# A scan kernel with an ELU layer behind it: B and C turned on VectorE instead of TensorE, one load for exp(cum), and other PSUM banks for the quarters of a product

## The chip, the cores and the metric

The kernel runs on one core of a Trainium2 chip. The core has five engines, each with a queue of its own that it works off in order: TensorE (PE in the profile; PEld is its weight load), VectorE (DVE), ScalarE (ACT), GpSimd (POOL) and SyncE (SP), which here only issues transfers. Products are written to PSUM, eight banks of 512 float32 values for each of 128 partitions; everything else lies in SBUF. The metric is the time of one execution on the device in microseconds (us).

## The reference

The input is `x` (4 batches, 8 heads, 768 positions, 32 channels), a decay `a` for each position, and `B` and `C` (16 states for each position). A scan runs along the positions, by chunks; its output of 3072 rows and 256 columns goes through two matrix products with an ELU between them. The weights come as float64.

```python
cum = np.cumsum(la, axis=-1)
L = np.exp(cum[:, :, :, None] - cum[:, :, None, :]) * causal
CB = np.einsum('bhin,bhjn->bhij', Cc, Bc)
y_intra = np.einsum('bhij,bhjd->bhid', CB * L, xc)
y_inter = np.einsum('bhin,bhnd->bhid', Cc, state) * np.exp(cum)[:, :, :, None]
y[:, :, sl] = y_intra + y_inter
Bx = np.einsum('bhjn,bhjd->bhjnd', Bc, xc) * np.exp(cum[:, :, -1:] - cum)[..., None, None]
state = np.exp(np.sum(la, axis=-1))[:, :, None, None] * state + np.sum(Bx, axis=2)
# then, on y as 3072 x 256:
h = x @ w_in                                            # 256 -> 2048
g = np.where(h > 0.0, h, np.exp(np.minimum(h, 0.0)) - 1.0)
return g @ w_out                                        # 2048 -> 256
```

## The kernel before

**Groups.** The 3072 rows are worked in 12 groups n of 256 positions, all 8 heads at once; groups 2p and 2p+1 are the same stretch of two batches and make a pair. For each group SyncE loads B and C into one tile `bc` (`load_bc`, line 106: four loads, positions on the partitions, eight heads of 16 states along the row) and `x` (`load_x`). From a table in DRAM it spreads exp(cum) over the partitions (`spread_exp`, line 340, tile `ec`: eight loads, one a head) and cum itself (`spread_cum`, tile `L`).

**The scan of a group.** `scaled` (line 357) multiplies B by a decay for the state's update. `turn` (line 368) transposes B and C with four products against the identity on TensorE into two PSUM tiles (`ps_tb`, `ps_tc`); ScalarE copies B to `bt`, VectorE writes C masked by head to `ctm`; `turn_exp` (line 385) writes C times exp(cum) to `cts`. `scores` multiplies them, `weigh` applies L, `sums` and `states` carry the state on, `across` and `inside` make y, which ScalarE copies to `yT`.

**The two layers.** The first four groups use plain products (`l1`, line 583, and `l2`, line 707). From group 4 on the two groups of a pair are taken together, and seven products stand for eight, by sums and differences of quarters (Strassen's scheme in Winograd's form). For each pair n and each of eight column blocks i of the hidden layer, three functions (lines 659 to 691, products at line 655) do so:

- `front`: three products of 128 x 256; ScalarE copies the first one out of PSUM (`p_copy`, line 665). `front_sums`: two sums on VectorE (lines 673, 674).
- `mid`: two products, one sum on VectorE (line 682).
- `back`: two products, two sums (lines 689, 690).

The results fill two PSUM tiles c1 and c2, each of two halves of 256 columns and one bank in size. Every product takes two passes of TensorE, so that the profile counts two records a product. The queue `lag` holds finished tiles for the ELU: `begin_elu` is relu of the negated value on ScalarE (line 596), `elu` adds exp on ScalarE (line 603) and max(e - 1, h) on VectorE (line 605, tile `g`), after which the bank is free. `sum_t1` and `sum_t2` on GpSimd form the differences of the quarters of g that the second layer needs.

`second(n)` is the second layer of a pair as 56 steps of two products of 128 x 128 (line 759), with sums on VectorE and GpSimd at line 750. The loop over k (two for each i) sets the order by hand: while the first layer of pair n runs, `l2s(count)` takes that many steps of the second layer of pair n-2 and lays them between front, mid and back: four steps after front, two after mid, one after back. `scan_ahead(n, i)` puts in the scan of the pair to come.

**PSUM.** Seven banks are one ring (`ps_a`), from which scores, states, y, turns, c1, c2 and half of the second layer's tiles are taken in turn; the eighth holds the rest. A tool of the language adds the waits between engines, and for PSUM it adds them between any two accesses of different engines to one bank.

Of the kernel before, what the change touches and what calls it, by code (L numbers as in the profile page):

```python
# [16 lines left out]
P = 128  # L17
# [11 lines left out]
def kernel(  # L29
# [76 lines left out]
    def load_bc(n, c_queue=nc.sync):  # L106
        b, g = place(n)
        st.setdefault(n, {})["bc"] = raw.tile([P, 2, 2, NH, N], F32, tag="bc", name="bc", bufs=2)
        for u in range(2):
            sl = slice((2 * g + u) * P, (2 * g + u + 1) * P)  # L110
            for k, src in enumerate((B, C)):
                (nc.sync, c_queue)[k].dma_start(  # L112
                    out=st[n]["bc"][:, k, u], in_=src[b, :, sl, :].rearrange("h s n -> s h n"))
# [226 lines left out]
    def spread_exp(n):  # L340

        st.setdefault(n, {})["ec"] = ec = att.tile([P, 2, P], F32, tag="ec", name="ec", bufs=4)
        for h in range(NH):
            row = rows_of(n).start + NG * h
            nc.sync.dma_start(
                out=ec[N * h:N * (h + 1)].rearrange("n u i -> n (u i)"),
                in_=flat_exp[row:row + 1].to_broadcast([N, BLK]))
# [11 lines left out]
    def scaled(n, eng):  # L359
# [5 lines left out]
            out=sc, in0=s["bc"][:, 0],  # L365
            in1=factor.unsqueeze(3).to_broadcast([P, 2, NH, N]), op=ALU.mult)

    def turn(n):
# [8 lines left out]
        s["bt"] = att.tile([P, 2, P], F32, tag="bt", name="bt", bufs=3)  # L377
# [7 lines left out]
    def turn_exp(n):  # L385
# [3 lines left out]
        nc.vector.tensor_tensor(out=s["cts"], in0=s.pop("ct"), in1=s["ec"], op=ALU.mult)  # L389
# [270 lines left out]
    def front(n, i):  # L660
# [5 lines left out]
        part_product(c2[:, 1], s_in[0][:, i], t[:, 1], True)  # L666
        part_product(c2[:, 0], a21[:, i], t[:, 0])
        open_[n, i] = c1, c2, copy

    def front_sums(n, i):  # L670
        c1, c2, copy = open_[n, i]
        u = conv.tile([P, 2, BLK], F32, tag="mag", name="u_sum")
        nc.vector.tensor_tensor(out=u[:, 0], in0=c2[:, 1], in1=copy, op=ALU.add)
        nc.vector.tensor_tensor(out=u[:, 1], in0=c2[:, 0], in1=u[:, 0], op=ALU.add)
        open_[n, i] = c1, c2, u

    def mid(n, i):
# [3 lines left out]
        part_product(c1[:, 1], s_in[1][:, i], y_sums[n][:, 2])  # L681
        nc.vector.tensor_tensor(out=c2[:, 1], in0=c1[:, 1], in1=u[:, 1], op=ALU.add)  # L682

    def back(n, i):
        c1, c2, u = open_.pop((n, i))
        b22 = yT[n // 2][:, 1, 1].rearrange("p u i -> p (u i)")
        part_product(c1[:, 1], a22[:, i], y_sums[n][:, 3])
        part_product(c2[:, 0], s_in[2][:, i], b22)
        nc.vector.tensor_tensor(out=c1[:, 1], in0=c1[:, 1], in1=u[:, 0], op=ALU.add)  # L689
        nc.vector.tensor_tensor(out=c2[:, 0], in0=c2[:, 0], in1=u[:, 0], op=ALU.add)  # L690
        lag.append((n, i, c1))
# [8 lines left out]
    def l2(n, j, half=None):  # L700
# [10 lines left out]
        if j == MC // 2 - 1 and half != 0:  # L711
            ob = ffn.tile([P, 2, DM], F32, tag="ob", name="ob")
# [11 lines left out]

    def sum_t1(n, i, eng=nc.gpsimd):
        b12 = g_of[n + 1, i][:, 0]
        eng.tensor_tensor(out=b12, in0=b12, in1=g_of[n, i][:, 0], op=ALU.subtract)  # L727

    def sum_t2(n, half):
        for i in range(4 * half, 4 * half + 4):  # L730
            t2_of[n, i] = ffn.tile([P, BLK], F32, tag="t2", name="t2", bufs=4)
            sub(t2_of[n, i], g_of[n + 1, i][:, 1], g_of[n + 1, i][:, 0])
# [3 lines left out]
    def second(n):  # L736
# [6 lines left out]
        for half in range(2):  # L743
# [8 lines left out]
            for r, a in enumerate((a11, a12, s1, s2, s3, a22, s4)):  # L752
                pool, tag = (p_a, "a") if (7 * half + r) % 2 else (p_o, "o")
                ps = pool.tile([P, 2, P], F32, tag=tag, name="ps_o")
                for i in chunk:
                    A, B = g_of[n, i], g_of[n + 1, i]
                    b = (A[:, 0], A[:, 1], B[:, 0], t2_of[n, i], A[:, 0], A[:, 1], B[:, 1])[r]
# [7 lines left out]
                if r == 0:  # L765
                    nc.scalar.copy(out=p1, in_=ps)
                    for i in chunk:
                        sub(g_of[n, i][:, 0], t2_of[n, i], g_of[n, i][:, 0])
                    if half:
                        add(c11, c11, p1)  # L770
                elif r == 1:
                    add(c11, ps, c11 if half else p1)
                    for i in chunk:
                        sub(g_of[n, i][:, 1], g_of[n, i][:, 1], t2_of[n, i])
# [139 lines left out]
    for s, (n, i) in enumerate((  # L914
# [14 lines left out]
        if s == 4:  # L929
            scaled(2, nc.gpsimd)  # L930
        if s == 5:
            turn(2)
            first_exp(2)
            turn_exp(2)
# [32 lines left out]
    def scan_ahead(n, i):  # L967
# [6 lines left out]
        if 4 <= m < NP and n % 2 == 0:  # L974
# [11 lines left out]
            if i in (5, 7):  # L986
                turn(m + i // 7)
                turn_exp(m + i // 7)
        if 4 <= m < NP and n % 2 == 1:
            if i == 0:  # L990
                scaled(m, nc.gpsimd)
                scaled(m + 1, nc.gpsimd)
            for k in (i,) if m == 4 else (i, i + 1) if i % 2 == 0 else ():
# [17 lines left out]
    for n in (2, 3):  # L1011
        for i in range(8):
# [11 lines left out]
            if n == 2:  # L1024
# [3 lines left out]
                if i == 1:  # L1028
                    scaled(3, nc.gpsimd)
                    turn(3)  # L1030
# [20 lines left out]
    for n in range(4, NP, 2):  # L1051
# [14 lines left out]
        for k in range(16):  # L1066
# [18 lines left out]
            elif m and i == 5:  # L1085
                l2s(2)
                mid(n, i)
                states(m)
                l2s(2)
                back(n, i)  # L1090
                states(m + 1)
                next_elu()
                begin_elu()
            else:
                mid(n, i)
                if i == 0 and n > 4:
                    store(n - 4, 0)
                    store(n - 4, 1)
                l2s(2)
                back(n, i)  # L1100

# [7 lines left out]
                next_elu()  # L1109
# [54 lines left out]
```

## Time and profile before

| | us |
|---|---|
| median of three runs (lowest, highest) | 366.25 (365.03, 367.19) |
| span of the profiled execution, first to last instruction | 362.9 |
| runs' median less this span | 3.35 |
| busy in it: TensorE | 354.3 |
| VectorE | 242.2 |
| GpSimd | 227.1 |
| ScalarE | 200.7 |

The profile shows one execution. The runs are timed on the device from outside, so that a few microseconds lie around the span. Stages, by the span: start and first groups to about 27 us, groups with plain first layer to 53, plain second and first layer to 117, the four pairs (n = 4, 6, 8, 10) to 334, and the second layer of the last pair to the end. In a row of the profile, `out<-in` are tiles, then shapes as partitions x elements, the count, busy time, the mean of one in ns, and the idle time of the engine before them with what ended it. A line of the chain has its start, its length and what ran.

### The profile page before, as it was taken

How to read it: one execution, taken by the hardware profiler on the slowest of the kernel's cores; microseconds unless marked ns; L12 is line 12 of the kernel's file. 1: busy time of each engine (PE TensorE's matmuls, PEld its weight loads, DVE VectorE, ACT ScalarE, POOL GpSimd, SP SyncE). 2: the span in 40 equal slices, each digit the busy share in tenths (PEclk: the TensorE clock that was granted, in tenths of full speed). 3: DMA queues.
4: the chain of work that ended last, by engine and by line, in shares of the span. 5: the costliest groups of instructions: out<-in, count | busy, mean ns of one | idle time of the engine just before them, and what ended most of it. 6: DMA issues, size and time to landing. Idle time of an engine off the chain costs nothing.

```text
span 362.9 us, 10146 instructions
## 1 busy us (share of the span) xinstructions
PE 354.3 (98%) x3978; PEld 316.9 (87%) x3978; DVE 242.2 (67%) x547; ACT 200.7 (55%) x499; POOL 227.1 (63%) x366
## 2 busy tenths in 40 slices
PE   8899999999999999999999999999999999999996
PEld 5578778888888998898999998999989999999995
DVE  4989887972697668784567684666685666666212
ACT  4858969767435567635485735386735352534100
POOL 4454443663567896679457578567587555456893
PEclk9999999999999999999999999999999999999999
DMA  8877995563050560053530045540000100000001
GB/s 155 203 203 147 240 308 141 66 116 63 3 116 19 65 85 12 4 115 48 96 65 2 3 95 68 93 72 0 3 2 4 58 2 0 3 0 32 29 2 58
DMA packets 96239, 25.33 MB, mean 70 GB/s; under 512 B 77312, under 2 KB 92096, under 8 KB 96192
## 3 DMA queue, kind: packets, MB, share of 16 engines
q1 hardware_dynamic: 94016, 24.49, 33.0%
q8 instruction: 31, 0.51, 0.6%
q10 hardware_dynamic: 2176, 0.20, 0.4%
q14 instruction: 16, 0.13, 0.1%
HBM read 21.33 MB, written 3.34 MB: 68 GB/s over the span
## 4 chain that ended last, share of the span: by engine, by line
PE 81%; DVE 7%; ACT 3%; DMA 3%; SPq 2%; issue 2%; POOL 1%; ACTq 0%; DVEq 0%
PE ps_o L759 32%; PE ps_h L655 25%; PE ps_h L583 10%; PE ps_o L707 8%; SPq L112 2%; PE ps_g L459 1%; DMA w<-in_moe_w_in_dram 1%; DVE g L605 1%; PE ps_y L553 1%; ACT e L596 1%; PE ps_st L489 1%; ACT e L603 1%; DMA flat<-F 1%; DVE mag L183 1%; PE ps_y L534 1%
## 5 line engine op out<-in xcount | busy, mean ns | idle before, releaser
L596 ACT ACTIVATE e<-ps_h 128x512 f32<-128x512 f32 x96 | 56.5, 588 | 93.1 <-DVE ps_h L689 71.2
L605 DVE SCALAR_TENSOR_TENSOR g<-e,ps_h 128x512 f32<-128x512 f32 x96 | 65.3, 681 | 39.2 <-ACT e L603 35.8
L759 PEld LDWEIGHTS ps_o<-w_out,g 128*128 128x128 f32 x640 | 80.3, 192 | 3.3 <-issue 0.5
L759 PE MATMUL ps_o<-w_out,g 128*128 128x128 f32 x640 | 81.4, 275 | 0.0
L727 POOL TENSOR_TENSOR g<-g 128x256 f32<-128x256 f32 x34 | 24.8, 729 | 67.1 <-DVE g L605 67.1
L583 PE MATMUL ps_h<-yT,w_in 128*128 128x256 f32 x256 | 60.6, 383 | 2.5 <-POOL w_in L200 1.8
L603 ACT ACTIVATE e<-e 128x512 f32<-128x512 f32 x96 | 60.9, 634 | 2.2
L583 PEld LDWEIGHTS ps_h<-yT,w_in 128*128 128x128 f32 x256 | 47.8, 190 | 10.6 <-POOL w_in L200 2.8
L759 PE MATMUL ps_o<-w_sum,g 128*128 128x128 f32 x320 | 43.0, 275 | 0.0
L759 PEld LDWEIGHTS ps_o<-w_sum,g 128*128 128x128 f32 x320 | 41.1, 192 | 1.4
L439 ACT ACTIVATE L<-L,ncum 128x64 f32<-128x64 f32 x160 | 41.0, 338 | 0.0
L655 PE MATMUL ps_h<-y_sum,w_in 128*128 128x256 f32 x128 | 38.6, 383 | 0.7 <-DVE ps_h L682 0.7
L655 PE MATMUL ps_h<-y_sum,w_sum 128*128 128x256 f32 x128 | 38.5, 382 | 0.5 <-DVE g L605 0.5
L655 PE MATMUL ps_h<-yT,w_in 128*128 128x256 f32 x128 | 38.8, 385 | 0.0
L444 POOL TENSOR_SCALAR_AFFINE_SELECT L<-L 64x512 f32<-64x512 f32 x40 | 27.3, 682 | 13.1 <-ACT L L439 11.8
L707 PE MATMUL ps_o<-w_out,g 128*128 128x256 f32 x128 | 30.8, 383 | 0.0
L655 PEld LDWEIGHTS ps_h<-y_sum,w_sum 128*128 128x128 f32 x128 | 23.9, 190 | 5.3 <-DVE g L605 1.3
L723 POOL TENSOR_TENSOR g<-t,g 128x256 f32<-128x256 f32 x40 | 27.9, 729 | 0.8 <-PE ps_o L759 0.8
L723 POOL TENSOR_TENSOR t<-g 128x256 f32<-128x256 f32 x40 | 28.1, 736 | 0.2
L723 POOL TENSOR_TENSOR g<-g,t 128x256 f32<-128x256 f32 x40 | 27.9, 730 | 0.2
L707 PEld LDWEIGHTS ps_o<-w_out,g 128*128 128x128 f32 x128 | 23.7, 190 | 3.4 <-POOL L L444 0.2
L689 DVE TENSOR_TENSOR ps_h<-ps_h,u_sum 128x256 f32<-128x256 f32 x32 | 13.7, 429 | 18.3 <-PE ps_h L655 18.3
(109 smaller groups left out, 538.3 us busy)
## 6 DMA issues: line engine op xcount, KB each, us to landing
L<-flat SPq DMA_DIRECT2D x20, 256.0 KB, 5.3
w<-in_moe_w_in_dram SPq DMA_DIRECT2D x8, 512.0 KB, 5.2
w<-in_moe_w_out_dram SPq DMA_DIRECT2D x8, 512.0 KB, 6.1
xr<-in_x_dram SPq DMA_DIRECT2D x24, 128.0 KB, 3.4
out_dram<-c_sum SPq DMA_DIRECT2D x10, 256.0 KB, 2.1
bc<-in_B_dram SPq DMA_DIRECT2D x24, 64.0 KB, 4.4
bc<-in_C_dram SPq DMA_DIRECT2D x22, 64.0 KB, 3.4
ec<-flat_exp SPq DMA_DIRECT2D x72, 16.0 KB, 1.7
```

The lines of the kernel that those rows point to most:

```text
L439: nc.scalar.activation(L[:, h, u], L[:, h, u], ACT.Exp, bias=ncum[:, u, row:row + 1])
L444: nc.gpsimd.affine_select(out=part, in_=part, pattern=[[0, 4], [0, 2], [1, Q]], compare_op=ALU.is_ge, fill=0.0, base=0, channel_multiplier=-1)
L583: nc.tensor.matmul(out=ps[:, j], lhsT=w_in[:, k, m * P:(m + 1) * P], rhs=yT[n // 2][:, k, n % 2].rearrange("p u i -> p (u i)"), start=(k = ...
L596: nc.scalar.activation(begun[0], lag[0][2], ACT.Relu, scale=-1.0)
L603: nc.scalar.activation(e, e, ACT.Exp, scale=-1.0)
L605: nc.vector.scalar_tensor_tensor(out=g_of[n, i], in0=e, scalar=1.0, in1=ps, op0=ALU.subtract, op1=ALU.max)
L655: nc.tensor.matmul(out=out, lhsT=lhsT, rhs=rhs, start=first, stop=True, skip_group_check=True)
L689: nc.vector.tensor_tensor(out=c1[:, 1], in0=c1[:, 1], in1=u[:, 0], op=ALU.add)
L707: nc.tensor.matmul(out=o_of[n][:, ts], lhsT=g_of[n, j][:, m % 2, ts * P:(ts + 1) * P], rhs=w_out[:, m], start=(m == 0 and ts == 0), stop=( ...
L723: nc.gpsimd.tensor_tensor(out=out, in0=in0, in1=in1, op=ALU.subtract)
L727: eng.tensor_tensor(out=b12, in0=b12, in1=g_of[n, i][:, 0], op=ALU.subtract)
L759: nc.tensor.matmul(out=ps[:, ts], lhsT=b[:, ts * P:(ts + 1) * P], rhs=a[:, i], start=(i == chunk[0] and ts == 0), stop=(i == chunk[-1]), s ...
```

## The change

It has four parts.

1. **Turning.** For groups 2 to 11, B and C are loaded so that each run of 8 positions x 16 states of one head is a row of 512 bytes on one partition, and one VectorE operation (`turn_square`, a transpose within squares of 32 x 32) for each of B and C makes the turned tile `bct` out of it. B in the old layout is loaded as well, for `scaled`. `mask_heads` and `turn_exp` follow as VectorE steps of their own, read SBUF in place of PSUM, and are spread over the steps by `turn_part`. Groups 0 and 1 keep `turn`.
2. **exp(cum)** comes by one load a group in place of eight.
3. **Banks.** front's second product goes to the second half of c1 in place of c2; mid's second and back's first product go to c2, the sums write the other way, and back's two sums become one over the whole of c2. c1 is then whole after mid. `quarters` tells which half of g is which quarter.
4. **Order.** c1's ELU begins after mid and ends before back, c2's begins after back.

```diff
+        if n > 1:
+            st[n]["b"] = raw.tile([P, 2, NH, N], F32, tag="b", name="b_tok", bufs=2)
+            for u in range(2):
+                sl = slice((2 * g + u) * P, (2 * g + u + 1) * P)
+                nc.sync.dma_start(
+                    out=st[n]["b"][:, u], in_=B[b, :, sl, :].rearrange("h s n -> s h n"))
...
+            for k, src in enumerate((B, C)):
+                for m in range(2):
+                    nc.sync.dma_start(
+                        out=squares[:, k, m],
+                        in_=src[b, m:NH:2, g * BLK:(g + 1) * BLK, :].rearrange(
+                            "q (c t) n -> q c (t n)", t=8))
+            return
...
-        for h in range(NH):
-            row = rows_of(n).start + NG * h
-            nc.sync.dma_start(
-                out=ec[N * h:N * (h + 1)].rearrange("n u i -> n (u i)"),
-                in_=flat_exp[row:row + 1].to_broadcast([N, BLK]))
+        nc.sync.dma_start(
+            out=ec.rearrange("p u i -> p (u i)"),
+            in_=flat_exp[rows_of(n)].unsqueeze(1).to_broadcast([NH, N, BLK]))
...
+    def turn_square(n, k):
...
+        nc.vector.transpose(
+            out=s["squares"][:, k].rearrange("p u i -> p (u i)").rearrange("p (c t) -> p t c", t=8),
+            in_=s["bc"].rearrange("p k u h n -> p k (u h n)").rearrange(
+                "p k (m t n) -> p k t m n", m=2, n=N)[:, k])
...
+    def turn_part(n, part):
+        if part < 2:
+            turn_square(n, 1 - part)
+        elif part == 2:
+            mask_heads(n)
+        else:
+            turn_exp(n)
...
         copy = conv.tile([P, BLK], F32, tag="sgn", name="p_copy")
         nc.scalar.copy(out=copy, in_=c1[:, 0])
-        part_product(c2[:, 1], s_in[0][:, i], t[:, 1], True)
-        part_product(c2[:, 0], a21[:, i], t[:, 0])
+        part_product(c1[:, 1], s_in[0][:, i], t[:, 1])
+        part_product(c2[:, 1], a21[:, i], t[:, 0], True)
...
-        nc.vector.tensor_tensor(out=u[:, 0], in0=c2[:, 1], in1=copy, op=ALU.add)
-        nc.vector.tensor_tensor(out=u[:, 1], in0=c2[:, 0], in1=u[:, 0], op=ALU.add)
+        nc.vector.tensor_tensor(out=u[:, 0], in0=c1[:, 1], in1=copy, op=ALU.add)
+        nc.vector.tensor_tensor(out=u[:, 1], in0=c2[:, 1], in1=u[:, 0], op=ALU.add)
...
-        part_product(c1[:, 1], s_in[1][:, i], y_sums[n][:, 2])
-        nc.vector.tensor_tensor(out=c2[:, 1], in0=c1[:, 1], in1=u[:, 1], op=ALU.add)
+        part_product(c2[:, 0], s_in[1][:, i], y_sums[n][:, 2])
+        nc.vector.tensor_tensor(out=c1[:, 1], in0=c2[:, 0], in1=u[:, 1], op=ALU.add)
+        lag.append((n, i, c1))
...
-        part_product(c1[:, 1], a22[:, i], y_sums[n][:, 3])
-        part_product(c2[:, 0], s_in[2][:, i], b22)
-        nc.vector.tensor_tensor(out=c1[:, 1], in0=c1[:, 1], in1=u[:, 0], op=ALU.add)
-        nc.vector.tensor_tensor(out=c2[:, 0], in0=c2[:, 0], in1=u[:, 0], op=ALU.add)
-        lag.append((n, i, c1))
+        part_product(c2[:, 0], a22[:, i], y_sums[n][:, 3])
+        part_product(c2[:, 1], s_in[2][:, i], b22)
+        nc.vector.tensor_tensor(
+            out=c2, in0=c2, in1=u[:, 0].unsqueeze(1).to_broadcast([P, 2, BLK]), op=ALU.add)
         lag.append((n + 1, i, c2))
...
-            ob = ffn.tile([P, 2, DM], F32, tag="ob", name="ob")
+            ob = ffn.tile([P, 2, DM], F32, tag="ob", name="ob", bufs=1)
...
-            if i in (5, 7):
-                turn(m + i // 7)
-                turn_exp(m + i // 7)
+            if i > 2:
+                turn_part(m + i // 6, i % 3)
...
                 mid(n, i)
...
+                begin_elu()
                 l2s(2)
+                next_elu()
                 back(n, i)
-
+                begin_elu()
...
                 l2s(1)
-                next_elu()
-                begin_elu()
```

## The prediction

> **What bounds the kernel now.** I read the page first: engine shares, then the chain that ended last.
>
> ```profile
> PE 354.3 (98%) x3978; PEld 316.9 (87%) x3978; DVE 242.2 (67%) x547; ACT 200.7 (55%) x499; POOL 227.1 (63%) x366
> ...
> PE 81%; DVE 7%; ACT 3%; DMA 3%; SPq 2%; issue 2%; POOL 1%; ACTq 0%; DVEq 0%
> ```
>
> TensorE (PE) is busy almost throughout and carries 81% of the chain; the shares of VectorE, ScalarE and GpSimd are an average with slack. A busy PE is not yet a PE at its pace, so the chain in order of time comes next, for one turn of the loop over i in the stage of pairs (117 to 334 us, 32 turns).
>
> ```profile
> 180.41 1.30 PE ps_h L655 x6
> 181.71 1.78 PE ps_o L759 x16
> 183.50 0.87 PE ps_h L655 x4
> 184.36 0.89 PE ps_o L759 x8
> 185.25 0.87 PE ps_h L655 x4
> 186.56 1.30 PE ps_h L655 x6
> ```
>
> A turn is 6.15 us (186.56 - 180.41): front's three products 1.30 (0.43 each, two records a product), eight L759 products 1.78, mid's two 0.87, four L759 0.89, back's two 0.87, two L759 0.44. The parts add up to the turn, so PE has no gap in it. Anything put between two PE products here lengthens the kernel one for one. What stands around PE is in the timeline.
>
> ```profile
> 178.94 0.60 PE L655 MATMUL ps_h<-y_sum,w_in 128*128 128x256 f32 x2
> 179.38 0.59 PE L655 MATMUL ps_h<-yT,w_sum 128*128 128x256 f32 x2
> 179.58 0.43 DVE L689 TENSOR_TENSOR ps_h<-ps_h,u_sum 128x256 f32<-128x256 f32 x1 [0.89 <-PE ps_h L655]
> 180.04 0.60 ACT L596 ACTIVATE e<-ps_h 128x512 f32<-128x512 f32 x1 [2.23 <-DVE ps_h L689]
> 180.25 0.60 PE L655 MATMUL ps_h<-yT,w_in 128*128 128x256 f32 x2
> 180.67 0.63 ACT L603 ACTIVATE e<-e 128x512 f32<-128x512 f32 x1
> 180.69 0.59 PE L655 MATMUL ps_h<-y_sum,w_sum 128*128 128x256 f32 x2
> 181.21 0.58 ACT L596 ACTIVATE e<-ps_h 128x512 f32<-128x512 f32 x1
> 181.69 0.36 ACT L665 COPY p_copy<-ps_h 128x256 f32<-128x256 f32 x1
> ```
>
> The front starts at 180.25, its second product at 180.69. The copy of the first product (L665) stands on ScalarE behind relu, exp, relu and runs from 181.69 to 182.05: 1.36 us after the second product began. Today nobody on PE needs it before mid, 1.78 us of products later; that cover is what the change has to keep or lose. Three more views give prices: the timeline at a turn of B and C, the timeline at a wait, and two groups of the page or of the list by line.
>
> ```profile
> 135.85 0.38 PE L374 MATMUL ps_tb<-ident,bc 128*128 128x128 f32 x2
> 136.06 0.38 PE L374 MATMUL ps_tc<-ident,bc 128*128 128x128 f32 x2
> ...
> 142.20 0.70 PE L655 MATMUL ps_h<-y_sum,w_in 128*128 128x256 f32 x2 [0.67 <-DVE ps_h L682]
> ```
>
> ```profile
> L665 ACT COPY p_copy<-ps_h 128x256 f32<-128x256 f32 x32 | 11.8, 369 | 6.2 <-PE ps_h L655 6.1
> ...
> L750 DVE TENSOR_TENSOR c_sum<-ps_o,c_sum 128x256 f32<-128x256 f32 x20 | 8.4, 421 | 12.2 <-POOL c_sum L750 10.5 <-PE ps_o L759 1.7
> ```
>
> The copy takes 0.37 us in the mean; some of VectorE's L750 sums sat waiting for GpSimd, 10.5 us in all. The next PE work after the four transposes starts at 136.28, so a group's transposes take 0.43 us of PE. After a wait PE restarts 0.53 us before its next product (142.20, 142.73) where 0.43 is usual: 0.1 us of uncovered weight load per wait.
>
> **What the Trainium skill says.** "PSUM — Partial Sum Buffer", section "PSUM bank collisions raise a hardware error": two engines must not touch one bank in the same 32 partitions at once, whatever the addresses, so waits belong to the bank. The trace of before doesn't show such a wait apart (its c1[:, 0] products wait for the copy of the same half), but the changed program's waits follow it. "Perfetto Trace Analysis", section "Optimizing Tensor Performance", Matmuls: rotate independent groups through different banks so that evacuation overlaps the next matmuls; the trace agrees: copy in c1, second product in c2, no gap. "VectorE: DVE Perf Modes", section "The three transpose paths": VectorE turns 32x32 blocks only, 311 ns for 128x128 bf16. No square transpose is in the trace.
>
> **The change part by part.** Sums are made against the profiled execution: span 362.9 us. The runs' median is 366.25, 3.35 more, for what lies around the span; I add that at the end.
>
> 1. Banks in front. Before: c1[:, 0], ScalarE copies it, c2[:, 1], c2[:, 0]. After: c1[:, 0], copy, c1[:, 1], c2[:, 1]. The second product now writes the bank that ScalarE reads. In the changed program's queue this product waits for p_copy (L707 there), in all 32 fronts, and nothing stands on PE between first product and wait. Behind it on PE queue two front products and everything later.
> When does the copy end? ScalarE's order in after: relu(c1), exp(c1), relu(c2), copy. VectorE's: mid's sum, g(c1), back's sum. Count from the start of mid's second product: mid's sum starts at 0.63 (183.77 to 184.40 in the timeline), 0.43 long: 1.06. relu 0.03+0.60: 1.69. exp 0.03+0.63: 2.35. g(c1) starts 2.38; back's one sum of 128x512 stands behind it and starts 0.60 later (an independent VectorE operation overlaps by 0.08): 2.98. Its length isn't shown; L605 and L381 of that size take 0.68, two halves 0.86 at most: I take 0.68: 3.66. relu(c2) at 3.69, copy 0.48 after it (181.21 to 181.69): 4.17, ends 4.54, PE goes on at 4.59.
> PE reaches that product after 0.43+0.89+0.87+0.44+0.43 = 3.06. Stall 1.53 us. The 1.36 above, with the old order of the ELU, bears out its size.
> The 32 fronts (n = 4, 6, 8, 10, eight i each; all but n=10 have scan work for the next pair): i=1 to 4 always, 16; i=0 for n=6, 8, 10, since the ring runs on from the pair before; i=5 to 7 for n=10; i=7 for n=8, whose inside falls in an even step: 23 ordinary x 1.53 = 35.2. Three (i=6 with scan work) lack the two L759 products before the front: 1.97 x 3 = 5.9. Three (i=5) have 2 to 3 us of scores, sums and L759 ahead, only the turn-round is left: 0.2+0.37+0.05 = 0.62 x 3 = 1.9. Two (i=7, n=4 and 6) follow the yT copies on ScalarE, six of 0.32: 1.7 x 2 = 3.4. The first of all, behind one ELU: 1.3. Sum 47.7. The p5 copy falls between relu and exp about five times, 0.3 each: 1.5. Restart 0.1 x 32 = 3.2. Together 52.4. Mid's products gain waits too: c1[:, 0] for L715 and c2[:, 0] for L716, which read the same banks. VectorE ends L716 about 1.5 us after the second front product starts, PE comes there at 0.87+1.78 = 2.65: covered, with 1.1 us to spare, so nothing is taken; without that margin it would add one for one. What is late next is the whole of PE: the stall comes back each turn, and VectorE, ScalarE and GpSimd wait with it. The last L759 stage (334 us to the end) has no front and keeps its length.
>
> 2. PE transposes gone for groups 2 to 11: 10 x 0.43 = -4.3. The stalls of PE that came right after turns or late copies (0.83, 0.43, 0.36, 0.21, 0.15 by the starts of PE's records) disappear in the larger ones: -2.0. The bt copies (0.36, ScalarE, after exps) were hidden.
>
> 3. Squares: 20 more VectorE operations of 256 elements. The nearest row is 0.42 (L673); bounds 0.31 and 1.0. In odd steps they stand behind back's sum, inside the new stall. In even steps VectorE has front's sums to about 1.5, g to 2.1, up to two L750 sums to 3.0, and mid's sum is due at 3.72: 0.45 fits, 1.0 would cost some 0.3 us in the six even steps that hold one (two per scanned pair), +2. Before the pairs (40 to 80 us, VectorE 17 to 18.6 of 20) four squares, 1.7 us, less one cts moved to GpSimd: I take +0.5, bounds -0.4 and +1.7. A square that waited for a late load would hold VectorE; loads are issued at k=0 and 1, used from k=3, over 6 us later, and land in 3.7 us.
>
> 4. SyncE: per group 4 loads and 8 of ec become 6 and 1. Fewer issues by queue order, B loaded twice; they end earlier (L112 at 25 us held the queue 4.30 us, but PE was without gaps from 27.5 to 38.2). Nothing. ob single: its two uses lie 30 us apart.
>
> 5. back's two sums become one (0.86 to 0.68) and c1's ELU starts at mid: counted in 1.
>
> Sum: 362.9 + 52.4 - 4.3 - 2.0 + 0.5 = 409.5, and 3.35 outside the span: 413.
>
> **Rivals.** A, ordinary but short stall: ScalarE reaches the copy at once, as in the i=5 fronts; 32 x (0.62+0.1) = 23, so 362.9+23-5.8+3.35 = 383. For it: ScalarE is only 55% busy. Against: relu(c2) stands ahead of the copy and depends on back's sum.
> B, not slower: the copy is covered. It decides at one place, between front's first and second product: with 1.5 us of other PE work there the wait costs nothing and 362.9-5.8+3.35 = 360.5 remains. For it: PE hides the same copy today. Against: the queue has no such work there.
> C, longer: VectorE also falls behind. Its L750 sums waited 10.5 us for GpSimd in all before (hidden); those that stand between mid's sum and g(c1) would lengthen the new ring, and slow squares add 2: 413+10+2 = 425.
>
> **How the numbers follow.** Likeliest case 0.83, A 0.05, B 0.03, C 0.09. In the likeliest the stall is uncertain by some 0.3 us per front (0.1 for the unshown back sum's length, 0.2 for what stands before g(c1) on VectorE), 10 us in all, and the unknown squares by -1 to +3: its own range is 401 to 424. The range of 400 to 425 takes in the nearer half of C; A, B and the rest of C, about 0.13, and the tails of the likeliest stay out. About 0.5% (1.8 us) is what this measurement can tell from no change. Faster 0.03 (B), same 0.01, slower 0.96.
>
> **What would show it.** Right: the second front product (y_sum,w_sum) waits for ACT p_copy, some 1.5 us, about 30 times, a turn of 7.6 to 7.8 us, PE busy well under 98%, only the 8 PE transposes of groups 0 and 1 left, 20 square transposes on VectorE of about 0.42. Wrong: turns near 6.15 us (B), waits near 0.6 (A), PE waiting for VectorE's L724 or for L801 (C), or a square that waits for its load.

## The result and the profile after

The changed kernel takes 418.5 us (417.4 to 419.4) where the kernel before, on the same chip, takes 365.6 (364.1 to 367.2): a ratio of 1.145, 95% interval 1.141 to 1.149. The forecast was 413, with a range of 400 to 425. Its profiled execution took 418.49 us and has a span of 416.8.

First the page of the changed kernel, engine shares and chain:

```profile
PE 359.8 (86%) x3938; PEld 312.2 (75%) x3938; DVE 250.1 (60%) x534; ACT 200.3 (48%) x489; POOL 231.2 (55%) x367
...
PE 51%; ACT 21%; DVE 14%; SPq 5%; issue 5%; DMA 3%; POOL 0%; ACTq 0%; DVEq 0%
```

TensorE's share of the span fell from 98% to 86% and its share of the chain from 81% to 51%; ScalarE and VectorE, 3% and 7% of the chain before, now carry 35%. No engine is full any more, so the bound is a ring of waits. The chain in order of time shows one turn of it in the stage of pairs (start, length, what):

```profile
204.97 1.13 PE ps_h L697 x4
206.10 1.78 PE ps_o L810 x16
207.89 0.88 PE ps_h L697 x4
...
208.79 0.44 DVE ps_h L724
...
209.26 0.61 ACT e L638
...
209.89 0.64 ACT e L645
...
210.55 0.69 DVE g L647
211.24 0.62 DVE ps_h L732
...
211.88 0.60 ACT e L638
212.48 0.27 ACT p_copy L707
...
212.79 1.13 PE ps_h L697 x4
```

A turn is 7.82 us (212.79 - 204.97), where it was 6.15. It goes from the front's last two products, eight of the second layer (L810) and mid's two over mid's sum (L724), relu and exp of c1 (L638, L645), g (L647), back's sum (L732) and relu of c2 (L638) to the copy (L707). Then the next front may go on. The list of waits (us in total, times, longest) and the timeline at the end of this turn show the place:

```profile
PE ps_h L697 <- ACT p_copy L707: 43.9, 32, 1.9
```

```profile
210.79 0.60 PE L697 MATMUL ps_h<-yT,w_in 128*128 128x256 f32 x2
211.16 0.69 DVE L732 TENSOR_TENSOR ps_h<-ps_h,u_sum 128x512 f32<-128x512 f32 x1
...
211.88 0.60 ACT L638 ACTIVATE e<-ps_h 128x512 f32<-128x512 f32 x1 [1.36 <-DVE ps_h L732]
212.38 0.37 ACT L707 COPY p_copy<-ps_h 128x256 f32<-128x256 f32 x1
...
212.79 0.70 PE L697 MATMUL ps_h<-y_sum,w_sum 128*128 128x256 f32 x2 [1.40 <-ACT p_copy L707]
```

The front's first product starts at 210.79, the second at 212.79 instead of 0.43 us later: a stall of 1.57 us. With 0.1 for the restart behind it, it is the 1.67 by which the turn is longer. All 32 fronts wait for the copy, 43.9 us in all; no such wait stood in the kernel before. The groups of the page's list show VectorE's new operation and the product that waits (count, then busy us and mean ns, then idle time before and what ended it):

```profile
L697 PE MATMUL ps_h<-y_sum,w_sum 128*128 128x256 f32 x128 | 41.3, 404 | 43.9 <-ACT p_copy L707 43.9
...
L413 DVE STREAM_TRANSPOSE bct<-bc 128x256 f32<-128x256 f32 x20 | 12.7, 633 | 0.0
```

A square transpose takes 0.63 us. Where the time went, by stage: the pairs are taken from the start of the first front to the start of the last record of a y_sum,w_sum product (us; the other kernels are told of below):

| kernel | up to the pairs | pairs | after them | span |
|---|---|---|---|---|
| before | 117.40 | 214.14 | 31.34 | 362.89 |
| changed | 118.31 | 266.51 | 31.97 | 416.78 |
| banks alone | 117.20 | 265.97 | 31.36 | 414.54 |
| turning alone | 117.57 | 218.82 | 31.93 | 368.31 |
| changed, wait covered | 117.24 | 221.56 | 31.94 | 370.75 |

Of the 53.9 us that the span grew by, 52.4 lie in the pairs.

### The profile page after: what moved, and what is told of

Read it like the earlier page. It is cut to its first block, busy times and chain, and to the rows that moved or that the text cites. A ratio compares the mean times of both kernels' runs of the same rounds, so it can differ in the third digit from the quotient of the medians.

```text
span 416.8 us, 9923 instructions
## 1 busy us (share of the span) xinstructions
PE 359.8 (86%) x3938; PEld 312.2 (75%) x3938; DVE 250.1 (60%) x534; ACT 200.3 (48%) x489; POOL 231.2 (55%) x367
## 4 chain that ended last, share of the span: by engine, by line
PE 51%; ACT 21%; DVE 14%; SPq 5%; issue 5%; DMA 3%; POOL 0%; ACTq 0%; DVEq 0%
PE ps_o L810 20%; PE ps_h L697 15%; ACT e L638 9%; PE ps_h L625 7%; PE ps_o L749 6%; ACT e L645 5%; DVE g L647 5%; DVE ps_h L732 5%; DVE ps_h L724 3%; DMA w<-in_moe_w_in_dram 2%; ACT p_copy L707 2%; ACT L L481 2%; SPq L129 2%; PE ps_y L595 1%; DMA flat<-F 1%
## 5 line engine op out<-in xcount | busy, mean ns | idle before, releaser
L638 ACT ACTIVATE e<-ps_h 128x512 f32<-128x512 f32 x96 | 57.0, 594 | 135.2 <-DVE ps_h L724 69.6
L647 DVE SCALAR_TENSOR_TENSOR g<-e,ps_h 128x512 f32<-128x512 f32 x96 | 65.4, 683 | 46.2 <-ACT e L645 45.9
L810 PEld LDWEIGHTS ps_o<-w_out,g 128*128 128x128 f32 x640 | 80.3, 192 | 3.2 <-issue 0.5
L810 PE MATMUL ps_o<-w_out,g 128*128 128x128 f32 x640 | 81.5, 276 | 0.0
L697 PE MATMUL ps_h<-y_sum,w_sum 128*128 128x256 f32 x128 | 41.3, 404 | 43.9 <-ACT p_copy L707 43.9
L697 PEld LDWEIGHTS ps_h<-y_sum,w_sum 128*128 128x128 f32 x128 | 21.7, 189 | 58.3 <-ACT p_copy L707 49.4
L645 ACT ACTIVATE e<-e 128x512 f32<-128x512 f32 x96 | 60.9, 635 | 2.0
L810 PE MATMUL ps_o<-w_sum,g 128*128 128x128 f32 x320 | 43.7, 279 | 0.1
L810 PEld LDWEIGHTS ps_o<-w_sum,g 128*128 128x128 f32 x320 | 41.9, 195 | 1.6 <-PE ps_o L810 0.2
L715 DVE TENSOR_TENSOR u_sum<-ps_h,p_copy 128x256 f32<-128x256 f32 x32 | 13.6, 424 | 38.7 <-PE ps_h L697 38.5
L724 DVE TENSOR_TENSOR ps_h<-ps_h,u_sum 128x256 f32<-128x256 f32 x32 | 13.8, 433 | 36.0 <-PE ps_h L697 36.0
L765 POOL TENSOR_TENSOR t<-g 128x256 f32<-128x256 f32 x40 | 28.8, 752 | 0.3
L765 POOL TENSOR_TENSOR g<-t,g 128x256 f32<-128x256 f32 x40 | 27.8, 726 | 1.1 <-PE ps_o L810 1.1
L765 POOL TENSOR_TENSOR g<-g,t 128x256 f32<-128x256 f32 x40 | 27.8, 727 | 0.3
```

What stands on the lines that cost most here:

```text
L638: nc.scalar.activation(begun[0], lag[0][2], ACT.Relu, scale=-1.0)
L645: nc.scalar.activation(e, e, ACT.Exp, scale=-1.0)
L647: nc.vector.scalar_tensor_tensor(out=g_of[n, i], in0=e, scalar=1.0, in1=ps, op0=ALU.subtract, op1=ALU.max)
L697: nc.tensor.matmul(out=out, lhsT=lhsT, rhs=rhs, start=first, stop=True, skip_group_check=True)
L724: nc.vector.tensor_tensor(out=c1[:, 1], in0=c2[:, 0], in1=u[:, 1], op=ALU.add)
L765: nc.gpsimd.tensor_tensor(out=out, in0=in0, in1=in1, op=ALU.subtract)
```

## The experiments

Theory: the front's second product waits for ScalarE's copy in its own bank. Rivals: the turning, or the new place of the ELU, or VectorE's sums. Medians stand beside those of the kernel before on the same chip.

**One part at a time.** The diff falls into two halves: the banks (p_a quarters, `front`, `mid`, `back`, `quarters`, places of the ELU) and the turning (square loads, `turn_square`, `mask_heads`, one load of `ec`, the single `ob`). Each was put on the kernel before alone.

> Only the banks of the quarters, the single sum in back and the order of the ELU; B and C turned by TensorE as before. Theory: the whole loss and the 4.3 us of transposes, 418 to 424 us, with some 32 waits of y_sum,w_sum for p_copy. Rival one: about 366 us.

Measured 416.48 us beside 364.9, ratio 1.140 (1.135 to 1.146): +51.6. It is a little below the expected range; the wait is there 32 times, 43.3 us. The banks alone are nearly the whole loss.

> Only the turning on VectorE and the single load of exp(cum); banks, sums and the order of the ELU as before. Theory (the second front product waits for the copy): the stall is gone, 366 - 4.3 for the transposes + 0.5 to 3 for the first groups, 361 to 366 us. Rival one (the added VectorE work costs the time): over 400 us.

Measured 372.17 beside 364.9, ratio 1.021 (1.016 to 1.026): +7.3, where no change or a gain was expected. That miss is followed up below. The two add up to 58.9, more than the 52.9 of both together: with the ring idle for 1.57 us per turn, part of what the turning costs is hidden in it.

**Where the wait bites.** In the changed kernel the last two products of the front were swapped, so that the one in c1's bank comes third:

```diff
-        part_product(c1[:, 1], s_in[0][:, i], t[:, 1])
         part_product(c2[:, 1], a21[:, i], t[:, 0], True)
+        part_product(c1[:, 1], s_in[0][:, i], t[:, 1])
```

> The changed kernel with front's last two products swapped: the one into c2 runs while ScalarE copies c1. Theory: 0.43 us of each stall is filled, 32 x 0.43 = 14 us, 418.5 - 14 = 404.5 us (401 to 408). Rival one, and rival two (the new order of the ELU costs the time): 418 us, since VectorE's and ScalarE's queues are the same.

403.84 beside 364.9, ratio 1.106 (1.101 to 1.111): +38.9, where the changed kernel has +52.9. One product of 0.43 us moved ahead of the wait takes 13.9 us off, 0.43 in each of 32 turns. That is what filling a wait of a ring does; a cost that sat elsewhere would not have moved.

**What the copy waits behind.** In the changed kernel the copy stands behind relu of c2. Here c2's ELU begins only after the next front has issued its copy:

```diff
                 back(n, i)
-                begin_elu()
...
                     front(n, i)
+                    if lag and not begun:
+                        begin_elu()
```

> The changed kernel with c2's relu put behind the next front's copy on ScalarE. Theory: the copy no longer waits for back's sum, only the turn-round of 0.65 us and 0.1 of restart are left in each of 32 fronts: 24 us in place of 55, 418.5 - 31 = 388 us (383 to 394). Rival two (c1's and c2's ELU come too late): c2's relu comes later still, 418 us or more.

391.42 beside 364.9, ratio 1.073 (1.067 to 1.079). The timeline of this kernel shows what is left:

```profile
211.50 0.60 PE L697 MATMUL ps_h<-yT,w_in 128*128 128x256 f32 x2
211.87 0.69 DVE L732 TENSOR_TENSOR ps_h<-ps_h,u_sum 128x512 f32<-128x512 f32 x1
212.14 0.37 ACT L707 COPY p_copy<-ps_h 128x256 f32<-128x256 f32 x1 [0.91 <-PE ps_h L697]
...
212.56 0.70 PE L697 MATMUL ps_h<-y_sum,w_sum 128*128 128x256 f32 x2 [0.46 <-ACT p_copy L707]
```

The copy starts while back's sum (211.87 to 212.56) is still running and no longer depends on it. The stall falls from 1.57 to 0.63 (212.56 - 211.50 - 0.43), the bare way from TensorE to ScalarE and back; a turn is 6.87 us (212.56 - 205.69). This is rival A's short stall.

**The new order of the ELU.** Changed kernel, with the calls of `begin_elu` and `next_elu` put back as they stand before (c1's after back):

```diff
                 mid(n, i)
-                begin_elu()
                 l2s(2)
-                next_elu()
                 back(n, i)
-                begin_elu()
                 l2s(1)
+                next_elu()
+                begin_elu()
```

> The changed kernel with the ELU issued in the order of the kernel before (c1's relu after back, not after mid), banks and turning as changed. My theory: the copy still stands behind relu, exp, relu on ScalarE, but back's one sum no longer stands behind g(c1) on VectorE, so the front waits about 0.96 us instead of 1.53: 27 fronts times 0.57 less, about 403 (399 to 408). Rival, that the new place of the ELU shortens the ring and only the bank lengthens it: at or above the changed kernel's 418.5.

401.69 beside 365.42, ratio 1.100 (1.094 to 1.106). The new order lengthens the ring by 17 us: it puts g of c1 (0.69) ahead of back's sum on VectorE. In the old order back's sum follows its products directly, and a typical stall is 0.97 instead of 1.57. So about a third of the loss comes from where the ELU stands, but only because the bank wait makes the ring the bound.

**Covering the wait.** The front issues first product, copy, the c2 product and one pair of second-layer products, and only then the one in c1's bank; c2's relu comes after the copy, as above. All products are the same, in another order:

```diff
-        part_product(c1[:, 1], s_in[0][:, i], t[:, 1])
         part_product(c2[:, 1], a21[:, i], t[:, 0], True)
...
+    def front_rest(n, i):
+        c1 = open_[n, i][0]
+        part_product(c1[:, 1], s_in[0][:, i], y_sums[n][:, 1])
...
                     front(n, i)
+                    l2s(1)
+                    front_rest(n, i)
```

Once with the banks alone, once with the whole change:

> The new banks alone (B and C turned by TensorE as before), but the front issues its c2 product and one pair of second-layer products between the first product and the one that shares c1's bank, and c2's relu is issued after the copy. It does the same products. My theory: with 0.89 us of other products in the gap the wait for the copy is covered, the turn comes back to about 6.15 to 6.3 us, and the whole to 362 to 369. Rival one, that the new banks cost by VectorE's later sums or by the products of mid and back and not by the copy's wait: 380 or more. Rival two, half covered: 0.3 us left per front, about 375.

> The whole changed kernel with the front's wait covered (the front issues its c2 product and one pair of second-layer products between the first product and the one that shares c1's bank; c2's relu after the copy). All work is done. My theory: of the 53 us that the change cost, only the turning's 7 and the 4 that the cover of the new banks leaves remain, 373 (368 to 378), about 45 us less than the changed kernel. Rival, that turning and banks hinder each other beyond their sum once TensorE has no slack: over 380.

Banks covered: 369.47 beside 365.42, ratio 1.012 (1.008 to 1.016), half a microsecond above the range expected. Whole change covered: 371.67 beside 364.56, ratio 1.019 (1.017 to 1.022). In its waits TensorE stands for the copy twice, 0.6 us, instead of 32 times, 43.9. Its timeline shows the order that does it:

```profile
183.18 0.60 PE L697 MATMUL ps_h<-yT,w_in 128*128 128x256 f32 x2
...
183.61 0.59 PE L697 MATMUL ps_h<-y_sum,w_in 128*128 128x256 f32 x2
183.81 0.37 ACT L707 COPY p_copy<-ps_h 128x256 f32<-128x256 f32 x1 [0.91 <-PE ps_h L697]
...
184.04 0.61 PE L813 MATMUL ps_o<-w_out,g 128*128 128x128 f32 x4
...
184.49 0.60 PE L697 MATMUL ps_h<-y_sum,w_sum 128*128 128x256 f32 x2
...
189.33 0.60 PE L697 MATMUL ps_h<-yT,w_in 128*128 128x256 f32 x2
```

The copy ends at 184.18, 0.31 us before the product that shares its bank starts, and the turn is 6.15 us again (189.33 - 183.18), as in the kernel before. Of the 52.9 us, 45.8 come back by the order of TensorE's queue and of one relu. So nearly all that the banks cost is a gap in TensorE's queue that other products can fill. Of the 4.0 us that the covered banks still lose, the profiled execution shows 4.1 in the pairs, where TensorE now waits for g three times (1.4 us); the rest was not traced to a cause. No version here beats the kernel before.

**Why the turning costs 7 us.** Turning alone saves TensorE 40 products and still loses. Its trace has two kinds of new stops on TensorE in the pairs: before back's products, for mid's sum (5.1 us in eight places, one of 0.83 before the change), and in the midst of `inside`'s products (2.4 us in three places). The first was looked at with four kernels.

Squares alone: 20 unread square transposes added to the kernel before, TensorE turning as ever.

```diff
+            if i in (3, 4, 6, 7):
+                spare_square(m + i // 6, 1 - i % 3)
             if i in (5, 7):
                 turn(m + i // 7)
```

> The kernel before, with 20 square transposes of the loaded B and C added on VectorE at the places of the changed kernel (steps 3, 4, 9, 10 and i = 3, 4, 6, 7); their results are not read, and TensorE turns B and C as before. Theory one, the squares lengthen VectorE's queue so that mid's sum comes late for back's products: of the 9.7 us gross that turning cost alone (5.4 in the span and 4.3 of TensorE's work saved) they bear about 12.8 of 17.5 us of VectorE's added work, so +7 us, 372 (369 to 376). Theory two, the loss comes from the other parts (loads in squares, the mask and cts now read from SBUF): 364 to 367.

367.12 beside 365.42, ratio 1.005 (1.002 to 1.007). 12.8 us of VectorE work cost only 1.7, and TensorE's waits for mid's sum grew by 1.3 us: theory one, with its 7 us, falls.

Mask and cts on GpSimd (in the turning alone):

```diff
-        nc.vector.tensor_tensor(
+        nc.gpsimd.tensor_tensor(
...
-            turn_exp(n)
+            turn_exp(n, nc.gpsimd)
```

> The turning alone (372.2 before), with the mask and cts of groups 3 to 11 moved from VectorE to GpSimd; squares stay on VectorE. Theory one, the squares are the cause and mask and cts only add: 366 to 371. Theory two, mask and cts (0.87 and 0.70 us each from SBUF, where 0.68 and 0.41 were taken from PSUM) are the cause, since they stand before mid's sum in single steps: 361 to 365. Theory three, VectorE's load is not the cause (loads come late): 371 to 374; more than 374 if GpSimd falls behind with its own sums.

381.68 beside 365.42, ratio 1.045 (1.040 to 1.050), worse than every theory's figure but the last clause. The waits of this kernel say why: the masks stand in GpSimd's queue behind its sums, and the scores wait for them, 3.2 us at each of three places in the pairs.

```profile
PE ps_g L501 <- POOL ctm L421: 11.3, 4, 3.2
```

By its time this run doesn't tell whether VectorE's load was the cause; it shows that GpSimd had no room. But its trace has the first kind of stop, before back's products, down from 5.1 us in eight places to 1.2 in two, with the squares still on VectorE: so masks and cts bear a large part of that stop.

Two inputs in SBUF. In the kernel before, mask and cts read the turned C from PSUM. In the changed one all their operands lie in SBUF. The groups of the turning alone show both forms side by side:

```profile
L421 DVE TENSOR_TENSOR ctm<-bct,hmask 128x512 f32<-128x512 f32 x10 | 8.7, 868 | 0.0
...
L404 DVE TENSOR_TENSOR cts<-bct,ec 128x256 f32<-128x256 f32 x9 | 6.3, 699 | 0.0
...
L396 DVE TENSOR_TENSOR ctm<-ps_tc,hmask 128x512 f32<-128x512 f32 x2 | 1.4, 691 | 1.1 <-PE ps_tc L389 1.1
...
L404 DVE TENSOR_TENSOR cts<-ps_tc,ec 128x256 f32<-128x256 f32 x2 | 0.8, 421 | 0.3 <-ACT ec L372 0.3
```

One by one: four masks take 1.02 to 1.38 us, all beside GpSimd's differences (L765) or its sums of weights (L217), and six take 0.68 to 0.69; five cts take 0.67 to 1.18, all beside GpSimd work, and the four at 0.42 run alone. Company alone isn't enough, since five of the six short masks have some too. The order of starting decides. Beside all nine long operations a GpSimd operation had started first, and the VectorE operation ends about 0.55 us (masks) or 0.29 us (cts) after that one's end, most of its own length of 0.68 or 0.42. Of the five short masks with company, four started first, and then it is GpSimd that is stretched: L769 takes 1.04 instead of 0.73 three times, L217 1.66 instead of 1.27. Beside the fifth, one GpSimd operation was in its last 0.05 us, and the next takes 0.87 where most on its line (L673) take 0.46. The Trainium skill says this: "SBUF — State Buffer", section "Who interferes with whom", a VectorE instruction with two SBUF inputs contends with a GpSimd instruction that reads SBUF, since its second input comes by the port that the two share; that port is an exclusive lock, and the order of issue decides who is blocked; one with a single SBUF input, outside the two-port modes, doesn't contend. The traces agree: the same mask from PSUM, beside the same L765 (L723 in the kernel before), takes 0.68. GpSimd pays in the differences too: its longest t goes from 0.81 in the kernel before to 1.18. Two kernels tested what that costs: one that gives the kernel before SBUF operands, one that gives the turning alone PSUM operands.

```diff
-        s["ct"] = tc_
+        tc_sb = att.tile([P, 2, P], F32, tag="tcs", name="tc_sb", bufs=1)
+        nc.scalar.copy(out=tc_sb, in_=tc_)
+        s["ct"] = tc_ = tc_sb
```

> The kernel before, B and C turned by TensorE, with one more ScalarE copy (some 0.36 us, 12 times) that takes the turned C to SBUF, and mask and cts reading it there. My theory: the masks at about 139, 194 and 250 us and the cts behind them, which run beside GpSimd's differences, are stretched to 1.0 to 1.2 and 0.6 to 0.9 us, three TensorE waits before back's products get 0.7 to 0.9 longer each, 366.5 to 370. Rival, that operands in SBUF cost nothing and only the copy is added: 364.5 to 366, all masks at 0.68.

369.96 beside 364.56, ratio 1.016 (1.012 to 1.020): +5.4. The mean mask went from 0.68 to 0.83, the mean cts from 0.41 to 0.67, and the waits before back's products grew from 0.83 in one place to 2.9 in three. So the stretch is real and costs time, less the part, not known, of the twelve ScalarE copies.

```diff
-            s["bt"], s["ct"] = s["squares"][:, 0], s["squares"][:, 1]
+            s["ct"] = psum([P, 2, P], "ps_ct")
...
+            turn_square(n, 1)
             mask_heads(n)
             turn_exp(n)
```

> The turning alone (372.2 before), with C's square written to a PSUM bank and C's mask and cts reading it there, straight after it (as TensorE's turn had it); B's square stays in SBUF. Loads, squares and their number as in the turning alone. My theory now, that the turning loses time because VectorE's mask and cts have both inputs in SBUF and are stretched while GpSimd works (1.02 to 1.38 us against 0.68, 0.91 to 1.18 against 0.42, in the trace of the turning alone) and stretch GpSimd's sums too: mask at 0.68 to 0.70 and cts at 0.41 to 0.43 everywhere, and 363 to 367. Rival, that loads or the squares in the chain are the cause: 370 or more.

371.94 beside 364.56, ratio 1.019 (1.017 to 1.022): nothing gained, although every mask took 0.69 and every cts 0.41 as expected. So the stretch can't be the whole cause either. Its timeline, and that of the turning alone at the same place, tell what the theories missed. Turning alone:

```profile
139.21 1.15 DVE L421 TENSOR_TENSOR ctm<-bct,hmask 128x512 f32<-128x512 f32 x1
...
142.00 0.63 DVE L413 STREAM_TRANSPOSE bct<-bc 128x256 f32<-128x256 f32 x1
142.48 0.48 DVE L724 TENSOR_TENSOR ps_h<-ps_h,u_sum 128x256 f32<-128x256 f32 x1
...
143.02 0.70 PE L697 MATMUL ps_h<-y_sum,w_in 128*128 128x256 f32 x2 [1.50 <-DVE ps_h L724]
```

With C's square in PSUM:

```profile
140.02 0.45 DVE L414 STREAM_TRANSPOSE ps_ct<-bc 128x256 f32<-128x256 f32 x1
...
140.51 0.69 DVE L422 TENSOR_TENSOR ctm<-ps_ct,hmask 128x512 f32<-128x512 f32 x1
...
141.12 0.42 DVE L404 TENSOR_TENSOR cts<-ps_ct,ec 128x256 f32<-128x256 f32 x1
...
143.17 0.63 DVE L414 STREAM_TRANSPOSE bt<-bc 128x256 f32<-128x256 f32 x1
143.65 0.47 DVE L725 TENSOR_TENSOR ps_h<-ps_h,u_sum 128x256 f32<-128x256 f32 x1
...
144.18 0.70 PE L698 MATMUL ps_h<-y_sum,w_in 128*128 128x256 f32 x2 [1.97 <-DVE ps_h L725]
```

In the turn in which the mask of a pair's first group falls, VectorE's queue is full from the mask to mid's sum, in the kernel before too: there TensorE already waits for mid's sum (the forecast's line at 142.20, a stop of 0.83 us by the starts of the products). What is added there reaches TensorE, in part at least: the 0.48 of a spare square lengthened this stop by 0.26. In the turning alone the square adds 0.48 from start to start, the stretch 0.47, and cts, moved one step on, takes 0.33 away; together 0.6 of the 0.83 that the stop grew by. With C's square in PSUM the stretch is gone (-0.47), but C's square (0.49 from start to start) and cts (0.33) now stand there, and B's square of the next group (0.48) stays. Squares and stretch both lengthen the queue, at one place; elsewhere squares mostly fit in, as the 1.7 us for 20 of them in the kernel before says. How the 7 us split between squares and stretch over all places isn't settled by these runs. Late loads of B and C aren't among the causes: no square waited for its load (idle time before L413 in the turning alone: 0.0).

**Stops without a wait.** The second kind of stop was a surprise. The timeline of the turning alone at 275 us, and the DMA view's row for the queue that brings TensorE's instructions, as the counts below will show (packets, MB, share of the 16 engines' time):

```profile
276.63 1.02 PE L595 MATMUL ps_y<-M,xr 64*32 64x64 f32 x79
...
278.75 0.73 PE L595 MATMUL ps_y<-M,xr 64*32 64x64 f32 x49 [1.10 <-issue]
```

```profile
q8 instruction: 31, 0.51, 0.6%
```

TensorE stops after 79 of 128 records of small products, and the program has no wait there. Counting TensorE's records in each trace (products, weight loads and the semaphore instructions in its queue), the stops in `inside` come after 4033, 5313 or 6593 of them, within one:

| kernel | stops over 0.25 us in `inside`'s second products in the pairs, us | TensorE's records before the stop |
|---|---|---|
| turning alone | 0.43, 0.63, 1.30 | 4033, 5313, 6593 |
| whole change, covered | 0.78, 0.71, 1.86 | 4033, 5313, 6593 |
| turning, square in PSUM | 0.72, 0.49, 1.65 | 4033, 5313, 6593 |
| changed | 0.32, 1.84 | 5313, 6593 |
| before, banks alone, banks covered, spare squares, mask from SBUF | none | - |

The numbers are 1280 apart, five times 256. The queue q8 brought 31 transfers of 16,384 bytes for the 7,963 records of the turning alone: some 256 instructions of 64 bytes in each. The place where one such piece ends is called a border here. The other kernels with the turning stop at the same counts, and that of `copy_first` once more before the pairs, for 2.54 us after 2753 records, also a border (4033 less five times 256). In all 26 stops over 0.2 us of the nine kernels with the turning (that of the next experiment among them), TensorE goes on 1.2 to 1.6 us after the last transfer on q8 ended, however long the stop: it waits for instructions. In the turning alone the record 256 before a stop was reached 2.2 to 3.4 us earlier; in the kernel before the same two borders are 5.6 to 7.9 us apart in time, and TensorE doesn't stop. The last run shifted the stream by 96 instructions, without touching the stretches themselves:

```diff
     idle_product(4)
-    idle_product(3)
+    for _ in range(24):
+        nc.tensor.matmul(
+            out=ps_idle[0:32, 0, 0:4], lhsT=idle[0:32, 0:32], rhs=idle[0:32, 0:4],
+            start=True, stop=True)
+    idle_product(2)
```

> The turning alone (372.2 before), with 24 tiny idle products (96 more TensorE instructions) at the very start,[...] and one idle product there a little shorter. Nothing else changes. In the traces of the four kernels that have the turning, TensorE stops in the midst of inside's second products without any wait, always at its 4033rd, 5313th or 6593rd instruction, which are multiples of 256 apart, just after 16-KB transfers of instructions; in the kernel before, with 8 more TensorE instructions per group, it stops at none. My theory: TensorE uses up a piece of 256 instructions in these dense stretches faster than the next one is brought, when a piece also begins just before the stretch; shifting the stream by 96 puts the borders as they stand in the kernel before, so the three stops (0.43, 0.63, 1.30 us) vanish and the whole is about 2.4 us shorter: 369.8 (368.5 to 371). Rival, that the stops come from data of these stretches (M or xr late): they stay at the same products with about the same length, 372 (371 to 373.5).

371.29 beside 365.05, ratio 1.018 (1.016 to 1.020). By time alone it doesn't decide: +6.2 where the turning alone has +7.3 is a gain within the two intervals, and 371.29 lies in the rival's range. The places of the stops do. The three are gone; the timeline has the 128 records in one piece:

```profile
279.25 1.51 PE L599 MATMUL ps_y<-M,xr 64*32 64x64 f32 x128
```

A stop of 0.37 us now stands after 961 records, again at a border (961 + 12 times 256 = 4033), in an earlier `inside`. The rival falls: the stops follow the count of instructions, not the data. In the pairs the profiled execution gains 1.4 us (218.82 to 217.40), less than expected, since two waits of the front's second product for VectorE's g (0.52 and 0.39), which the kernel before had too (0.36 and 0.43) and the stops had hidden, come back. The start grew by 2.7, since the first first-layer product comes at 16.15 instead of 13.52.

## Why the prediction was right, and where its sum was off

Step 1 holds in its mechanism and nearly in its size. Forecast and measured: the turn 7.6 to 7.8, measured 7.82; the stall 1.53 with 0.1 of restart, measured 1.57 with 0.1; the wait in all 32 fronts, found 32 times; all the stalls with their restarts 52.4, about 52.5 by the starts of TensorE's records. Back's sum of 128x512, assumed at 0.68, takes 0.69. The banks alone cost 51.6, forecast 50.4 (52.4 less 2.0 for stalls that disappear in it). `copy_first`, `p3_first` and `old_order` moved the time by what the step's own terms say. Rival A's short stall is what remains when the copy gets clear of relu; rival B's cover works as it says, but the queue had none; rival C's longer ring did not come. The step rested on the Trainium skill's "PSUM — Partial Sum Buffer", "PSUM bank collisions raise a hardware error": the product that writes the other half of the bank does wait for the copy, 32 times. What the runs show is this wait of the program; no run leaves it out, so none shows a collision.

The span was forecast at 409.5 and came to 416.8, 7.3 more; 1.65 less outside it (1.7 instead of 3.35) leaves the 5.65 by which 418.5 exceeds 412.85, the forecast before rounding. The 3.35 set a median of three runs against the span of one execution that was faster than that median; where a run is listed with both its time and its span, 1.7 to 2.0 us lie between them. By stages against the table: 4.5 more in the pairs than the 47.8 that the forecast's terms give there (47.7 + 1.5 + 3.2 - 2.0, less six groups at 0.43), 2.1 more before them, 0.6 after.

Step 2, "PE transposes gone, -4.3", and step 3, "+0.5", are the terms whose sum failed, sign and all. On top of the banks they should have taken 3.8 off the span, and it grew by 2.2 (414.54 to 416.78); the turning alone should have gained some 4 and cost 7.3. In the pairs of the changed kernel TensorE's transposes are gone as forecast (2.6 us for six groups). But its products in `inside` take 2.5 us longer, by stops at borders of the instruction stream, which no step thought of. VectorE's part is hidden there: no product of back waits for mid's sum any more, behind the 1.57 us of each turn. In the turning alone it shows, and three things in step 3 bear on it. First, the price: square transposes take 0.63, where I took 0.42 from a row with other operands; that is inside my bounds of 0.31 and 1.0, but above the 0.45 that I said would fit. The price that the Trainium skill gives in "VectorE: DVE Perf Modes", "The three transpose paths", 0.31 for 128x128 in bf16, is half of it, for half the elements. Second, the operands: I priced mask and cts as unchanged, though the diff moves their input from PSUM to SBUF, and beside GpSimd they are stretched to as much as twice (mask) or nearly three times (cts) their length. Third, the place: I judged VectorE's slack in an ordinary turn and took the 0.83 stall at 141 us only for one that would disappear. In the changed kernel it does; in the turning alone it doubles. It was the sign that VectorE had no slack in just the turn in which the squares and masks are put. That the total came out near in spite of all this is in part luck: the turning is small beside the banks, most of its cost falls into their stall, and the 1.65 outside the span went the other way.

Before the pairs I had taken 1.2 off and 0.9 came on. Part of it is a wait of 1.4 us for group 2's mask (TensorE at 44.0). The turning alone has the same two squares ahead of this mask and doesn't wait there, so the squares by themselves don't explain it. The first first-layer product starts 0.8 us later as well, and since that differs by over 1 us between traces of kernels that don't differ there, I don't explain it either. Nor are the 0.6 us after the pairs explained.

Part of step 4 can be said to hold: SyncE's loads show as no wait on TensorE's path in the pairs. It wasn't tested on its own, and the single `ob` wasn't either.

## What to carry to other kernels

When two products of one PSUM bank have another engine's read between them, the reader's whole queue moves onto TensorE's path; put products of another bank, longer than that way (0.63 us here when the reader is free), between them, and the same banks cost little. Price an edit at the busiest turn of the loop, not the ordinary one, and take a stall that is already there as a sign that the engine it waits for has no slack. When work moves from TensorE to VectorE, look at where the operands of the following operations now lie.

## What was not expected of the hardware

- TensorE's instructions came in pieces of 256 (16 KB). In dense stretches of small products it ran out of them: stops of 0.2 to 2.5 us with no wait, each ending 1.2 to 1.6 us after a transfer of instructions did. 96 idle instructions moved them.
- A VectorE operation on two SBUF inputs that started behind a GpSimd operation took up to 1.39 us instead of 0.68 (128x512, in the changed kernel) and 1.50 instead of 0.42 (128x256, with the mask's input copied to SBUF). Where it started first, GpSimd's took 1.04 instead of 0.73. With one input in PSUM it took 0.68 and 0.41 in the same company.
- A square transpose of 128x256 in fp32 took 0.63 us into SBUF and 0.45 into PSUM.
